# Two column tiles of 64 in place of each whole matmul, in a retention and MLP kernel

## The chip, the cores and the metric

The kernel runs on one core of one Trainium2 chip. The metric is the device time of one execution in microseconds. Before the change the median is 307.2 us of three runs (306.94 to 307.8). The executions compared here are of the fast state (granted TensorE clock 1.00), but for e8, whose single run has no state. The experiments ran on three chips (e1 to e4, e5 to e8, e9 to e12), each with its own rounds of the kernel before beside them. A profile's span is about 1.8 us shorter than the time of the same execution.

## The reference

```python
def _attn_ref(q, k, v):                     # 8 batches, 8 heads, 576 positions, 64 per head
    scores = 1/np.sqrt(64) * np.matmul(q, k.transpose(0, 1, 3, 2))
    gamma = 1.0 - 2.0 ** (-5.0 - np.arange(H))
    Dmat = np.where(rel >= 0, gamma[:, None, None] ** rel, 0.0)     # rel = i - j
    return np.matmul(scores * Dmat, v)

def _moe_ref(x, w_in, w_out):               # 4608 tokens, 512 -> 2048 -> 512
    h = x @ w_in
    return (h * (1 / (1 + np.exp(-1.702 * h)))) @ w_out
```

The output of the first, as 4608 rows of 512, is the input of the second. Inputs and output are float32; the kernel's matmuls are in bf16.

## The kernel before

TensorE does the matmuls and writes them to PSUM, a memory in banks; ScalarE and VectorE read the banks out, and the program lets a new group into a bank only after that. Each matmul has a weight load of its own. The rows are cut into 36 units of 128, and four units make a chunk of 512 columns for the MLP. For each unit TensorE does four things besides the MLP: `inter` (the running state times q), `scores` (k times q inside the unit), `values` (masked scores times v) and `state` (k times v, for later units). The MLP of a chunk has an *up* phase of 16 groups of four matmuls, each group followed by a gelu on ScalarE, and a *down* phase of 16 steps of four matmuls. The attention of later units is placed inside the MLP phases of earlier chunks.

```python
def state_mm(u, bank, first):
    # [cut]
    for hp in range(HP):                                  # HP = 4 pairs of heads
        op("pe", lambda e, hp=hp: e.matmul(
            kb[:, hp, :], kq[sl][:, 0, P * hp : P * hp + P],
            vp[u % NVP][:, 2 * hp : 2 * hp + 2, :],
            start=(first and hp == 0), stop=True, skip_group_check=True),
           reads=[f"kq{sl}_0", f"vp{u % NVP}"], writes=[bank])

def scores(u, sb0=None):                                  # contraction over 64 rows: row tiles
    # [cut]
            e.matmul(by_pair(bank)[:, hp, :], qt[64 * hh : 64 * hh + 64, hp, :],
                     qt[64 * hh : 64 * hh + 64, HP + hp, :], skip_group_check=True)

def values(u, first=False):                               # 64 outputs each: column tiles
    # [cut]
            e.matmul(ob[64 * hh : 64 * hh + 64, hp, :], vp[u % NVP][:, 2 * hp + hh, :],
                     pm[u % 4][hh][:, hp, :], ...)

def up(c, f):
    bank = f"H{count['up'] % 2}"                          # two PSUM banks in turn
    count["up"] += 1
    hb = banks[bank].ap()
    for a in range(HP):
        op("pe", lambda e, a=a: e.matmul(
            hb, w_in_sb[:, a, P * f : P * f + P], xT[c % 3][:, a, :],
            start=(a == 0), stop=(a == HP - 1)), ...)
    op("act", lambda e: e.activation(gT[c % 2][:, f, :], hb, AF.Gelu_apprx_sigmoid), ...)

def block(m):                                             # two units inside an MLP phase
    inter(a); inter(b)
    scores(a + 2); scores(b + 2)
    scores_out(a + 2, 0)
    values(a); values(b)
    # [cut: copies out of PSUM, later loads]
```

A matmul instruction addresses the whole 128x128 array, or a part of it: 64 rows and 128 columns (scores, two row tiles), or 128 rows and 64 columns (values, two column tiles). These are three tiling modes.

## Time and profile before

| | before |
|---|---|
| time, median | 307.2 us |
| span of the profiled execution | 305.3 us |
| TensorE busy (PE) | 299.5 us, 98% |
| ScalarE busy (ACT) | 121.3 us, 40% |
| TensorE waits for others, in all | 3.2 us, the last of them near 17 us |
| changes of tiling mode (counted in the trace) | 72 |

These lines are from the page of the kernel before: the line of busy times (us, share of the span, instructions), the chain that ended last by engine, and groups of instructions (line, engine, operation, tiles, shapes, count; then busy us, mean ns of one; then the idle time before them and its releaser). PEld is the weight loads.

```profile
PE 299.5 (98%) x2152; PEld 149.7 (49%) x2152; DVE 131.7 (43%) x277; ACT 121.3 (40%) x214; POOL 113.0 (37%) x139
...
PE 94%; POOL 3%; DMA 2%; issue 0%; ACT 0%; DVE 0%; POOLq 0%
...
L455 PE MATMUL psH<-xT,w_in_sb 128*128 128x512 bf16 x512 | 115.5, 379 | 0.0
L486 PE MATMUL psH<-w_out_sb,gT 128*128 128x512 bf16 x512 | 115.3, 379 | 0.0
L460 ACT ACTIVATE gT<-psH 128x512 bf16<-128x512 f32 x128 | 76.4, 597 | 49.3 <-PE psH L455 49.3
...
L455 PEld LDWEIGHTS psH<-xT,w_in_sb 128*128 128x128 bf16 x512 | 42.4, 97 | 62.6 <-ACT gT L460 22.8
```

A matmul of 379 ns counts as busy from its first read to its modelled end, so neighbours overlap and 98% says little. What counts is the distance between starts. Read from the single instructions of the trace, that distance inside one mode is 216 ns at N=512, 109 at 256, 56 at 128 and 29 at 64. At a change of mode it is about 95 ns more. The next lines are from the chain of waits in order of time (start us, length us, what), one usual block with the MLP round it: inter (L396), scores (L415), values (L434), MLP (L455).

```profile
161.72 0.45 PE psO L396 x8
162.17 0.55 PE psS L415 x16
162.72 0.57 PE psO L434 x16
163.29 1.83 PE psH L455 x8
165.12 4.32 PE psH L486 x20
```

Eight inter matmuls take 0.45 us, which is 56 ns each. Sixteen scores take 0.55 and sixteen values 0.57 us, of which eight pairs of 56 ns explain 0.45: the rest is the change into that mode. The first eight MLP matmuls take 1.83 us where 8 x 216 ns is 1.73: a third change.

Two of the waits of TensorE in this kernel, both in the head (who waited for whom, us in total, times, longest):

```profile
PE psS L415 <- ACT qkT L331: 0.7, 2, 0.3
...
PE psS L326 <- DMA kq<-in_k_dram: 0.3, 1, 0.3
```

And the weight loads of four groups of the last up phase (timeline, engine PEld: start us, length us, what, idle time before it and its releaser):

```profile
279.15 0.55 PEld L455 LDWEIGHTS psH<-xT,w_in_sb 128*128 128x128 bf16 x4 [0.32 <-ACT gT L460]
280.01 0.55 PEld L455 LDWEIGHTS psH<-xT,w_in_sb 128*128 128x128 bf16 x4 [0.32 <-ACT gT L460]
280.87 0.55 PEld L455 LDWEIGHTS psH<-xT,w_in_sb 128*128 128x128 bf16 x4 [0.32 <-ACT gT L460]
281.74 0.55 PEld L455 LDWEIGHTS psH<-xT,w_in_sb 128*128 128x128 bf16 x4 [0.32 <-ACT gT L460]
```

Each group of four begins with a load that waits for a gelu (L460), because the group's PSUM bank has to be read out first; the group period is 0.86 us, 4 x 216 ns.

### The profile page before, as it was taken

To read this page: it belongs to the slowest core of one execution; us is meant where nothing else is said; L and a number is where in the kernel's file an instruction comes from. 1 tells how busy PE (TensorE), PEld (TensorE's weight loads), DVE (VectorE), ACT (ScalarE), POOL (GpSimd) and SP (SyncE) were. 2 spreads that over 40 slices of the span, in tenths; PEclk is the share of its full clock that TensorE was granted. 3 is DMA by queue.
4 is the path that set the end of the run, shared out by engine and by line. 5 is a ranking of instruction groups with operands and counts; after the bars stand their busy time and mean duration, and the time that the engine had idled before them with its cause. 6 is when DMAs were issued, how large, how long until landed. Compare 5 with 4: busy or idle time off the path is not lost.

```text
span 305.3 us, 5121 instructions
## 1 busy us (share of the span) xinstructions
PE 299.5 (98%) x2152; PEld 149.7 (49%) x2152; DVE 131.7 (43%) x277; ACT 121.3 (40%) x214; POOL 113.0 (37%) x139
## 2 busy tenths in 40 slices
PE   8799999999999999999999999999999999999996
PEld 3444688445544444354445444545444544453344
DVE  5781860418453554245454544425452635210000
ACT  8566346211146213631363136412651165116611
POOL 9799920735336454260428015601562000000000
DMA  9999999999999999992699879985989510010022
GB/s 143 191 207 192 187 206 137 135 168 243 166 188 171 123 193 207 151 137 75 162 147 137 107 140 147 157 111 104 175 147 96 121 50 2 34 71 34 0 55 85
DMA packets 118119, 40.45 MB, mean 132 GB/s; under 512 B 107024, under 2 KB 111376, under 8 KB 118096
## 3 DMA queue, kind: packets, MB, share of 16 engines
q0 software_dynamic: 80016, 22.55, 68.5%
q1 hardware_dynamic: 38080, 17.57, 24.8%
q8 instruction: 17, 0.28, 0.4%
q14 instruction: 6, 0.05, 0.1%
HBM read 36.70 MB, written 9.44 MB: 151 GB/s over the span
## 4 chain that ended last, share of the span: by engine, by line
PE 94%; POOL 3%; DMA 2%; issue 0%; ACT 0%; DVE 0%; POOLq 0%
PE psH L486 37%; PE psH L455 36%; PE psH L472 5%; PE psO L434 3%; PE psS L415 3%; PE psS L348 2%; DMA vn<-in_v_dram 2%; PE psS L486 2%; POOL kq L203 2%; PE psO L396 2%; PE psO L486 1%; PE psS L312 1%; PE psS L512 1%; PE psO L512 1%; POOL vp L303 0%
## 5 line engine op out<-in xcount | busy, mean ns | idle before, releaser
L455 PE MATMUL psH<-xT,w_in_sb 128*128 128x512 bf16 x512 | 115.5, 379 | 0.0
L486 PE MATMUL psH<-w_out_sb,gT 128*128 128x512 bf16 x512 | 115.3, 379 | 0.0
L460 ACT ACTIVATE gT<-psH 128x512 bf16<-128x512 f32 x128 | 76.4, 597 | 49.3 <-PE psH L455 49.3
L217 POOL DMA_DIRECT2D vn<-in_v_dram x39 | 33.5, 870 | 115.2 <-DMA qkT<-kq 115.2
L486 PEld LDWEIGHTS psH<-w_out_sb,gT 128*128 128x128 bf16 x512 | 48.3, 98 | 56.4 <-ACT gT L460 1.9
L455 PEld LDWEIGHTS psH<-xT,w_in_sb 128*128 128x128 bf16 x512 | 42.4, 97 | 62.6 <-ACT gT L460 22.8
L494 ACT ACTIVATE osb<-psH 128x512 f32<-128x512 f32 x32 | 19.1, 597 | 106.7 <-PE psH L486 106.7
L424 DVE TENSOR_TENSOR pm<-psS,mask 128x512 bf16<-128x512 f32 x64 | 41.3, 684 | 44.9 <-PE psS L415 44.9
L203 POOL DMA_DIRECT2D kq<-in_q_dram x39 | 34.7, 899 | 0.0
L203 POOL DMA_DIRECT2D kq<-in_k_dram x39 | 34.5, 893 | 0.0
L444 DVE TENSOR_TENSOR xT<-psO,gq 128x512 bf16<-128x512 f32 x36 | 23.5, 684 | 12.2 <-PE psO L434 11.4
L378 DVE TENSOR_TENSOR kvf<-psS,kvf 64x256 f32<-64x256 f32 x24 | 10.1, 422 | 25.5 <-PE psS L348 25.3
L303 DVE TENSOR_TENSOR vp<-vn,vfac 128x512 bf16<-128x512 f32 x29 | 18.8, 688 | 0.2
L472 PE MATMUL psH<-xT,w_in_sb 128*128 128x256 bf16 x128 | 14.5, 273 | 0.0
L376 DVE COPY kvf<-psS 64x256 f32<-64x256 f32 x12 | 5.1, 422 | 20.0 <-PE psS L348 19.9
L477 ACT ACTIVATE gT<-psH 128x512 bf16<-128x512 f32 x16 | 9.6, 597 | 8.6 <-PE psH L472 8.6
L472 PEld LDWEIGHTS psH<-xT,w_in_sb 128*128 128x128 bf16 x128 | 11.8, 98 | 2.2 <-issue 0.2
L415 PE MATMUL psS<-qkT 64*128 64x128 bf16 x288 | 12.1, 218 | 0.7 <-ACT qkT L331 0.7
L434 PE MATMUL psO<-pm,vp 128*64 128x128 bf16 x288 | 12.2, 223 | 0.5 <-DVE vp L303 0.5
L518 DVE COPY osb<-psS 128x256 f32<-128x256 f32 x1 | 0.4, 425 | 28.4 <-PE psS L512 28.4
L348 PE MATMUL psS<-vp,kq 128*128 128x128 bf16 x128 | 12.4, 219 | 0.3 <-POOL vp L303 0.3
L348 PEld LDWEIGHTS psS<-vp,kq 128*128 128x128 bf16 x128 | 9.3, 98 | 6.9 <-ACT kv L361 0.7
(62 smaller groups left out, 147.5 us busy)
## 6 DMA issues: line engine op xcount, KB each, us to landing
vn<-in_v_dram POOLq DMA_DIRECT2D x31, 256.0 KB, 5.2
out_dram<-osb SPq DMA_DIRECT2D x31, 256.0 KB, 2.3
kq<-in_k_dram POOLq DMA_DIRECT2D x31, 128.0 KB, 5.7
kq<-in_q_dram POOLq DMA_DIRECT2D x31, 128.0 KB, 5.5
w_in_sb<-in_moe_w_in_dram POOLq DMA_DIRECT2D x4, 512.0 KB, 9.5
w_out_sb<-in_moe_w_out_dram POOLq DMA_DIRECT2D x4, 512.0 KB, 14.8
out_dram<-osb SPq DMA_DIRECT2D x10, 128.0 KB, 2.3
vn<-in_v_dram POOLq DMA_DIRECT2D x8, 128.0 KB, 4.0
```

What stands on the lines that cost most here:

```text
L203: e.dma_start(kq[sl][p0 : p0 + n, i, :].rearrange("p (h d) -> p h d", d=DH), src[b, :, s0 : s0 + n, :].rearrange("h p d -> p h d"),)
L217: e.dma_start(vn[sl][p0 : p0 + n, :, :], v[b, :, s0 : s0 + n, :].rearrange("h p d -> p h d"),)
L348: op("pe", lambda e, hp=hp: e.matmul(kb[:, hp, :], kq[sl][:, 0, P * hp : P * hp + P], vp[u % NVP][:, 2 * hp : 2 * hp + 2, :], start=(first ...
L415: op("pe", lambda e, hp=hp, hh=hh, bank=bank: e.matmul(by_pair(bank)[:, hp, :], qt[64 * hh : 64 * hh + 64, hp, :], qt[64 * hh : 64 * hh + ...
L424: op("dve", lambda e: e.tensor_tensor(pm[u % 4][hh].ap(), by_pair(bank), m[:, None, :].to_broadcast([P, HP, P]), ALU.mult), reads=[bank, " ...
L434: op("pe", lambda e, hp=hp, hh=hh: e.matmul(ob[64 * hh : 64 * hh + 64, hp, :], vp[u % NVP][:, 2 * hp + hh, :], pm[u % 4][hh][:, hp, :], st ...
L444: op("dve", lambda e: e.tensor_tensor(xT[ch % 3][:, :, 128 * j : 128 * j + 128], by_pair(bank), gq[:, ty, :, :], ALU.mult), reads=[bank] + ...
L455: op("pe", lambda e, a=a: e.matmul(hb, w_in_sb[:, a, P * f : P * f + P], xT[c % 3][:, a, :], start=(a == 0), stop=(a == HP - 1)), reads=[f ...
L460: op("act", lambda e: e.activation(gT[c % 2][:, f, :], hb, AF.Gelu_apprx_sigmoid), reads=[bank], writes=[f"gT{c % 2}_{f}"])
L472: op("pe", lambda e, a=a, f=f, j=j: e.matmul(hb[:, j, :], w_in_sb[:, a, P * f : P * f + P], xT[c % 3][:, a, n], start=(a == 0), stop=(a == ...
L486: op("pe", lambda e, f=f: e.matmul(y, gT[c % 2][:, f, P * r : P * r + P], w_out_sb[:, f, :], start=(f == 0), stop=(f == NF - 1)), reads=[f ...
L494: op("act", lambda e: e.activation(osb[o].ap(), y, AF.Copy), reads=[bank], writes=[f"osb{o}"])
```

## The change

The intent: let every matmul but the scores use the mode in which values stands anyway, 128 rows by 64 columns. Then the mode changes only on the way into scores and out of them. A whole matmul becomes two, one for each half of the output rows, which run side by side.

```diff
+        HALVES = (slice(0, 64), slice(64, 128))
+
+        def mm(y, lhs, rhs, reads, bank, start, stop=True, **kw):
+            for r in HALVES:
+                op("pe", lambda e, r=r: e.matmul(
+                    y[r], lhs[:, r], rhs, start=start, stop=stop, skip_group_check=True, **kw),
+                   reads=reads, writes=[bank])
@@ state_mm
             for hp in range(HP):
-                op("pe", lambda e, hp=hp: e.matmul(
-                    kb[:, hp, :], kq[sl][:, 0, P * hp : P * hp + P],
-                    vp[u % NVP][:, 2 * hp : 2 * hp + 2, :],
-                    start=(first and hp == 0), stop=True, skip_group_check=True),
-                   reads=[f"kq{sl}_0", f"vp{u % NVP}"], writes=[bank])
+                mm(kb[:, hp, :], kq[sl][:, 0, P * hp : P * hp + P],
+                   vp[u % NVP][:, 2 * hp : 2 * hp + 2, :],
+                   [f"kq{sl}_0", f"vp{u % NVP}"], bank, first and hp == 0)
@@ up
             for a in range(HP):
-                op("pe", lambda e, a=a: e.matmul(
-                    hb, w_in_sb[:, a, P * f : P * f + P], xT[c % 3][:, a, :],
-                    start=(a == 0), stop=(a == HP - 1)),
-                   reads=[f"win{f // 4}"] + [f"xT{c % 3}_{j}" for j in range(4)],
-                   writes=[bank])
+                mm(hb, w_in_sb[:, a, P * f : P * f + P], xT[c % 3][:, a, :],
+                   [f"win{f // 4}"] + [f"xT{c % 3}_{j}" for j in range(4)],
+                   bank, a == 0, a == HP - 1)
```

(The transposes, inter, the half-width up, the down matmuls and the warm-up are rewritten in the same way.)

More of the change, by code (lines that the diff above doesn't have):

```diff
@@ L311, in transpose_pe @@
             for j in range(2 * HP):
-                op("pe", lambda e, j=j: e.matmul(
-                    t[:, j, :], kq[sl][:, j // HP, P * (j % HP) : P * (j % HP) + P], ident.ap(),
-                    is_transpose=True), reads=[f"kq{sl}_{j // HP}", "ident"], writes=[bank])
+                mm(t[:, j, :], kq[sl][:, j // HP, P * (j % HP) : P * (j % HP) + P], ident.ap(),
+                   [f"kq{sl}_{j // HP}", "ident"], bank, True, is_transpose=True)
             if eng == "act":
@@ L325, in transpose_half @@
             for j in range(HP):
-                op("pe", lambda e, j=j: e.matmul(
-                    t[:, j, :], kq[sl][:, i, P * j : P * j + P], ident.ap(),
-                    is_transpose=True), reads=[f"kq{sl}_{i}", "ident"], writes=[bank])
+                mm(t[:, j, :], kq[sl][:, i, P * j : P * j + P], ident.ap(),
+                   [f"kq{sl}_{i}", "ident"], bank, True, is_transpose=True)
             dst = qkT[u % NQT][:, HP * i : HP * i + HP, :]
@@ L394, in inter @@
             for hp in range(HP):
-                if kind < 2:
-                    op("pe", lambda e, hp=hp: e.matmul(
-                        ob[:, hp, :], kv[kind][c - 1][:, hp, :], qt[:, HP + hp, :],
-                        start=(first and hp == 0), stop=True, skip_group_check=True),
-                       reads=[f"kv{kind}_{c - 1}_0", f"kv{kind}_{c - 1}_1", f"qkT{u % NQT}q"],
-                       writes=[bank])
-                else:
-                    for b in range(2):
-                        op("pe", lambda e, hp=hp, b=b: e.matmul(
-                            ob[:, hp, 64 * b : 64 * b + 64], kv[b][3][:, hp, :],
-                            qt[:, HP + hp, 64 * b : 64 * b + 64],
-                            start=(first and hp == 0 and b == 0), stop=True, skip_group_check=True),
-                           reads=[f"kv{b}_3_0", f"kv{b}_3_1", f"qkT{u % NQT}q"], writes=[bank])
+                for b in (kind,) if kind < 2 else (0, 1):
+                    n = slice(0, P) if kind < 2 else HALVES[b]
+                    x = c - 1 if kind < 2 else 3
+                    mm(ob[:, hp, n], kv[b][x][:, hp, :], qt[:, HP + hp, n],
+                       [f"kv{b}_{x}_0", f"kv{b}_{x}_1", f"qkT{u % NQT}q"], bank,
+                       first and hp == 0 and n.start == 0)
         def scores(u, sb0=None):
@@ L454, in up @@
             for a in range(HP):
-                op("pe", lambda e, a=a: e.matmul(
-                    hb, w_in_sb[:, a, P * f : P * f + P], xT[c % 3][:, a, :],
-                    start=(a == 0), stop=(a == HP - 1)),
-                   reads=[f"win{f // 4}"] + [f"xT{c % 3}_{j}" for j in range(4)],
-                   writes=[bank])
+                mm(hb, w_in_sb[:, a, P * f : P * f + P], xT[c % 3][:, a, :],
+                   [f"win{f // 4}"] + [f"xT{c % 3}_{j}" for j in range(4)],
+                   bank, a == 0, a == HP - 1)
             op("act", lambda e: e.activation(gT[c % 2][:, f, :], hb, AF.Gelu_apprx_sigmoid),
@@ L471, in up_half @@
                 for a in range(HP):
-                    op("pe", lambda e, a=a, f=f, j=j: e.matmul(
-                        hb[:, j, :], w_in_sb[:, a, P * f : P * f + P], xT[c % 3][:, a, n],
-                        start=(a == 0), stop=(a == HP - 1)),
-                       reads=[f"win{f // 4}"] + [f"xT{c % 3}_{2 * half + j}" for j in range(2)],
-                       writes=[bank])
+                    mm(hb[:, j, :], w_in_sb[:, a, P * f : P * f + P], xT[c % 3][:, a, n],
+                       [f"win{f // 4}"] + [f"xT{c % 3}_{2 * half + j}" for j in range(2)],
+                       bank, a == 0, a == HP - 1)
             op("act", lambda e: e.activation(
@@ L485, in down @@
             for f in range(4 * s, 4 * s + 4):
-                op("pe", lambda e, f=f: e.matmul(
-                    y, gT[c % 2][:, f, P * r : P * r + P], w_out_sb[:, f, :],
-                    start=(f == 0), stop=(f == NF - 1)),
-                   reads=[f"gT{c % 2}_{f}", f"wout{f // 4}"], writes=[bank])
+                mm(y, gT[c % 2][:, f, P * r : P * r + P], w_out_sb[:, f, :],
+                   [f"gT{c % 2}_{f}", f"wout{f // 4}"], bank, f == 0, f == NF - 1)
             if s < 3:
@@ L511, in down_last @@
                 for f in range(NF):
-                    op("pe", lambda e, f=f, y=y, c0=c0, c1=c1: e.matmul(
-                        y, gT[c % 2][:, f, P * r : P * r + P], w_out_sb[:, f, c0:c1],
-                        start=(f == 0), stop=(f == NF - 1)),
-                       reads=[f"gT{c % 2}_{f}", f"wout{f // 4}"], writes=[bank])
+                    mm(y, gT[c % 2][:, f, P * r : P * r + P], w_out_sb[:, f, c0:c1],
+                       [f"gT{c % 2}_{f}", f"wout{f // 4}"], bank, f == 0, f == NF - 1)
                 o = osb[r][:, c0:c1]
@@ L527, in warm @@
             for _ in range(n):
-                op("pe", lambda e: e.matmul(
-                    banks["H1"].ap(), zero[:, 0:P], zero.ap(), start=True, stop=True),
-                   reads=["zero"], writes=["H1"])
+                mm(banks["H1"].ap(), zero[:, 0:P], zero.ap(), ["zero"], "H1", True)
         def head_in(u, eng, bank="S2"):
```

## The prediction

> **What bounds the kernel now.** TensorE. The page's busy line gives PE 299.5 of 305.3 us (98%); the chain of waits is 94% PE; the view of waits shows PE waiting for others 3.2 us in all, none of it after 18 us. The granted clock is 1.00. So the time is the sum of PE's start-to-start intervals, read from the trace's single instructions. Inside one tiling mode they are 216 ns for a 128x512 matmul, 109 for N=256, 56 for N=128, 29 for N=64: nothing is left between matmuls except where the mode changes.
>
> **Mode changes.** The trace has 72 changes between 128x128, 64x128 (scores) and 128x64 (values). At each the first start comes about 95 ns later than the interval of that size (152 ns instead of 56 from the last values matmul to the first MLP matmul), and the next start another 10 to 20 ns late. This agrees with the Trainium skill, "TensorEngine Tiling (Array Packing)", Key Properties: a change of mode drains TensorE.
>
> **What the change removes.** Afterwards only the 22 groups of scores stand in another mode: 44 changes stay, 28 go. Four of the 28 lie before 16 us, where PE waits for a DMA anyway; 24 lie on the chain: 24 x (96 + about 10) ns = 2.5 us. The usual block (inter, scores, values, MLP) loses one change of three.
>
> **What it adds.** Matmuls go from 2152 to about 3,730, with as many weight loads. Column tiles do run side by side: the values pairs start 3 ns apart and follow each other every 56 ns, as whole matmuls with N=128 do. So I expect 216 ns per pair at N=512, 109 at 256, 56 at 128: no loss. The same page says that column tiling switches Fast Weight Load off; the trace shows 64-column loads of 110 ns against 98 ns for 128-column ones, hidden at N=128. The 32 matmuls with N=64 (29 ns) may not hide theirs: at worst 56 ns per pair, +0.9 us; I take +0.4. The other engines' work does not change.
>
> The unproved part is the supply of instructions. A period of 15.7 us needs about 384 PE instructions, 25 per us (18.5 inside the MLP), twice as many as before. The trace of before shows 320 in 12.7 us at the head; with a queue of 64 filled beforehand (the Trainium skill, "TensorE: Matmul & The Clock Gate", opening table) that proves at least 20 per us, an estimate. Capped near that, the kernel would be tens of us slower; I give this, or a loss between concurrent 512-column streams, one chance in eight.
>
> **Predicted:** 307.2 - 2.5 + 0.4 = 305.1 us, range 303.8 to 308.0. Faster by over 2%: 0.02; within 2%: 0.85; slower: 0.13.
>
> **What the profile would show.** Right: MLP matmuls as 128x64 pairs, starts 3 ns apart and 216 ns per pair; the first MLP start after values 56 ns after the last values pair, not 152; 44 mode changes of about 95 ns; a block (inter to first MLP matmul) of about 1.56 us instead of 1.66; weight-load busy time up; ACT and DVE busy times unchanged.
>
> **What would make it wrong.** Pairs over 216 ns at N=512 (weight loads no longer hidden, or two streams sharing a read path); gaps with no semaphore behind them (instruction supply); N=64 or transposed pairs well over 56 ns; a lower granted clock[...].

## The result, and the profile after

| | before | after |
|---|---|---|
| time, median (range) | 307.4 us (306.94 to 307.8, 4 runs) | 306.92 us (306.4 to 307.21, 4 runs) |
| ratio, 95% interval | | 0.9983 (0.9961 to 1.0005) |
| span of the profiled execution | 305.3 us | 305.4 us |
| matmuls | 2152 | 3728 |
| changes of tiling mode | 72 | 44 |

A ratio is the mean time of one kernel's fast runs over that of the other's of the same rounds, so it is not quite the ratio of the medians. About 0.5 us was gained; 2.1 us had been forecast. From the page after, the busy times and the chain:

```profile
PE 297.3 (97%) x3728; PEld 167.7 (55%) x3728; DVE 131.7 (43%) x277; ACT 121.4 (40%) x214; POOL 113.3 (37%) x139
...
PE 72%; DMA 15%; POOL 12%; issue 1%; DVE 0%; SPq 0%; POOLq 0%
...
```

From the groups by form of the kernel after (columns as above; line 313 is the helper, 456 the gelu):

```profile
L313 PE MATMUL psH<-xT,w_in_sb 128*64 128x512 bf16 x1024 | 116.4, 381 | 0.1
L313 PE MATMUL psH<-w_out_sb,gT 128*64 128x512 bf16 x1024 | 115.5, 379 | 0.0
L456 ACT ACTIVATE gT<-psH 128x512 bf16<-128x512 f32 x128 | 76.5, 597 | 49.6 <-PE psH L313 49.6
L313 PEld LDWEIGHTS psH<-xT,w_in_sb 128*64 128x64 bf16 x1280 | 63.1, 109 | 57.0 <-ACT gT L456 21.6 <-ACT osb L486 2.2 <-DVE xT L442 0.6
```

The down matmuls (`w_out_sb`) keep their mean of 379 ns, the up matmuls (`w_in_sb`) have 381: the first hint. The chain by engine looks quite different (72% PE, where it was 94%). That is no statement about shares of cost: one wait for a DMA at 84 us makes the walk back through the chain leave TensorE there and follow the loads before it. The usual block, from the chain of waits:

```profile
162.22 0.45 PE psO L313 x16
162.67 0.55 PE psS L413 x16
163.22 0.57 PE psO L432 x16
163.79 6.06 PE psH L313 x56
```

The 28 pairs of the MLP after values now take 6.06 us, where 28 x 216 ns is 6.05; before it was 1.83 + 4.32 = 6.15 us. The change of mode between values and MLP is gone, as forecast. In single instructions, the first MLP start comes 56 ns after the start of the last values pair (155 before; the prediction's 152 was counted from the pair's second matmul), and the block from its first inter to the first MLP matmul takes 1.568 us (1.663 before).

The waits of TensorE for loads of q and k after:

```profile
PE psS L313 <- DMA kq<-in_k_dram: 1.2, 2, 0.8
...
PE psS L413 <- DMA qkT<-kq: 0.6, 1, 0.6
...
PE psS L313 <- DMA kq<-in_q_dram: 0.2, 1, 0.2
```

The largest sum misleads: the two waits for k (1.2 us, where 0.3 was) stand at 7.8 and 13.0 us, and at 17 us this execution is only 0.06 us behind that of before. The two that cost time are new: 0.16 us of idle time for q of unit 4 at 28.2 us (the start there is 0.33 us late) and 0.57 us for the transposed q and k of unit 13 at 84.0 us (0.74 us late). And the weight loads of the last up phase:

```profile
279.12 0.57 PEld L313 LDWEIGHTS psH<-xT,w_in_sb 128*64 128x64 bf16 x8 [0.31 <-ACT gT L456]
279.99 0.57 PEld L313 LDWEIGHTS psH<-xT,w_in_sb 128*64 128x64 bf16 x8 [0.29 <-ACT gT L456]
280.87 0.57 PEld L313 LDWEIGHTS psH<-xT,w_in_sb 128*64 128x64 bf16 x8 [0.31 <-ACT gT L456]
281.73 0.57 PEld L313 LDWEIGHTS psH<-xT,w_in_sb 128*64 128x64 bf16 x8 [0.29 <-ACT gT L456]
```

The group starts are now 0.87, 0.88 and 0.86 us apart, and the idle time before them alternates between 0.31 and 0.29 us. The single instructions of the trace (times in us) show what happens at such a load:

```
                          weight load that     its matmul   the next     distance
                          waited for ScalarE   starts       matmul
before, a group           87.665               87.680       87.897       217 ns
after, a group            87.359, 87.362       87.365       87.600       235 ns
after, the next group     88.222, 88.225       88.248       88.464       216 ns
```

Of the 431 up intervals at N=512 after 54 us, 39 are more than 10 ns too long after the change, and none before.

**Where the time went, by anchors.** ScalarE executes the same 212 activations in the same order in both kernels. Comparing their starts gives the lag of one kernel against the other at any place. The table adds the later experiments; each row is one profile against the first profile of before.

| profile | to 87.0 us | 87.0 to 275.0 us | 275.0 us to the last | sum |
|---|---|---|---|---|
| after | +0.56 | -0.62 | +0.16 | +0.09 |
| after, second profile (e1) | +0.39 | -0.62 | +0.16 | -0.08 |
| after, more banks (e2) | +0.56 | -1.23 | +0.02 | -0.65 |
| before, more banks (e3) | +0.42 | 0.00 | 0.00 | +0.42 |
| after, loads reordered (e4) | +0.02 | -0.62 | +0.15 | -0.44 |
| after, whole head (e5) | 0.00 | -0.62 | +0.16 | -0.46 |
| before, warm-up cut (e6) | +0.40 | 0.00 | 0.00 | +0.40 |
| whole head and more banks (e7) | -0.16 | -1.23 | +0.02 | -1.37 |
| after, last up whole (e8) | +0.54 | -0.62 | +0.23 | +0.15 |
| e7 with inter whole (e10) | +0.07 | +0.12 | +0.02 | +0.21 |
| e7 with state whole (e11) | +1.08 | +3.53 | +0.02 | +4.63 |
| e7 with loads reordered (e12) | +0.11 | -1.23 | +0.02 | -1.10 |

From 87 us on the numbers repeat to 10 ns from profile to profile; up to there (the head) kernels with the very same TensorE instructions differ by 0.4 us. Those 0.4 us are there at 17 us already: from 17 to 87 us e3 and e6 repeat the kernel before to 0.03 us, and only the kernels with column tiles differ, by -0.41 (e7) to +0.50 us (after), e10 and e11 with their added changes left aside. The second table splits the time from 86 us to the end by the distances between starts, in us.

| profile | changes of mode | cost of them, with the start after | late MLP starts |
|---|---|---|---|
| before | 35 | 3.89 | 0.00 |
| after | 22 | 2.51 | 0.85 |
| e2 | 22 | 2.51 | 0.13 |
| e10 | 35 | 3.90 | 0.13 |
| e11 | 64 | 7.26 | 0.13 |

The late starts that stay in e2 are those of the first down matmuls, which wait for a gelu too. So after 86 us 13 changes of mode went and saved 3.89 - 2.51 = 1.38 us, 106 ns each, exactly the price in the prediction; and 0.85 us of it was lost again in the MLP.

### The profile page after: what moved, and what is told of

Same layout as the page of the kernel before. It is cut to its first block, busy times and chain, and to the rows that moved or that the text cites. A ratio compares the mean times of both kernels' runs of the same rounds, so it can differ in the third digit from the quotient of the medians.

```text
span 305.4 us, 8273 instructions
## 1 busy us (share of the span) xinstructions
PE 297.3 (97%) x3728; PEld 167.7 (55%) x3728; DVE 131.7 (43%) x277; ACT 121.4 (40%) x214; POOL 113.3 (37%) x139
## 4 chain that ended last, share of the span: by engine, by line
PE 72%; DMA 15%; POOL 12%; issue 1%; DVE 0%; SPq 0%; POOLq 0%
PE psH L313 60%; DMA kq<-in_q_dram 9%; POOL kq L203 6%; PE psS L313 4%; DMA qkT<-kq 3%; POOL vn L217 3%; PE psO L313 3%; PE psO L432 2%; DMA vn<-in_v_dram 2%; PE psS L413 2%; POOL vp L303 1%; POOL w_out_sb L232 1%; POOL w_in_sb L226 0%; POOL iota_c L238 0%; DVE osb L508 0%
## 5 line engine op out<-in xcount | busy, mean ns | idle before, releaser
L313 PE MATMUL psH<-xT,w_in_sb 128*64 128x512 bf16 (+1 forms) x1280 | 131.0, 359 | 0.1
L313 PE MATMUL psH<-w_out_sb,gT 128*64 128x512 bf16 x1024 | 115.5, 379 | 0.0
L313 PEld LDWEIGHTS psH<-xT,w_in_sb 128*64 128x64 bf16 x1280 | 63.1, 109 | 57.0 <-ACT gT L456 21.6
L313 PEld LDWEIGHTS psH<-w_out_sb,gT 128*64 128x64 bf16 x1024 | 56.1, 110 | 48.6 <-ACT gT L456 1.9
L313 PEld LDWEIGHTS psS<-vp,kq 128*64 128x64 bf16 x256 | 10.3, 110 | 5.9 <-ACT kv L366 0.7
L413 PE MATMUL psS<-qkT 64*128 64x128 bf16 x288 | 12.2, 218 | 1.4 <-ACT qkT L338 0.7
L313 PE MATMUL psS<-vp,kq 128*64 128x128 bf16 x256 | 12.6, 220 | 0.2 <-POOL vp L303 0.2
L389 DVE TENSOR_TENSOR kv<-psS,kvf 64x256 bf16<-64x256 f32 x12 | 5.1, 422 | 16.2 <-PE psS L313 16.1
L386 DVE CAST kv<-kvf 64x256 bf16<-64x256 f32 x36 | 11.4, 317 | 1.2
```

The source lines that it names most:

```text
L313: op("pe", lambda e, r=r: e.matmul(y[r], lhs[:, r], rhs, start=start, stop=stop, skip_group_check=True, **kw), reads=reads, writes=[bank])
L386: op("dve", lambda e, d=dst, s=acc: e.tensor_copy(d, s), reads=[kfk, f"kv{kind}_{c}"], writes=[kvk])
L413: op("pe", lambda e, hp=hp, hh=hh, bank=bank: e.matmul(by_pair(bank)[:, hp, :], qt[64 * hh : 64 * hh + 64, hp, :], qt[64 * hh : 64 * hh + ...
```

## The experiments

My theory after reading the traces had two parts. W: in the up phase a group's first weight load waits for a gelu, and a 64-column load must stand longer ahead of its matmul than a whole one, so that a wait which had just been hidden shows. H or D: the head, up to about 84 us, is set by loads and copies, so that what TensorE saves there turns into waiting. The rival S: twice as many instructions are not supplied fast enough, or the two streams of a pair disturb each other.

**e1, the changed kernel again.** No edit.

> The changed kernel, unaltered, for a second profile and a tighter ratio. Three accounts of the 2 us that the prediction missed. (W) In the up phases a group's first weight load waits for the gelu of two groups earlier; a 64-column load needs about 25 ns before its matmul, a whole one about 13, and only about 15 ns of slack were there, so every second group of the seven later up phases loses 20 ns: I expect start intervals of about 235 ns again, some 30 to 55 of them, 0.6 to 1.1 us. (D) Loads from memory: the first profile had a 0.74 us wait for the transposed q and k of units 12 and 13 near 83 us and 0.33 us near 28 us. If this is the change's own doing, both waits stand here again at like size; if it is run-to-run scatter of the DMA, they move by several tenths. (S, rival) shortage of instructions: gaps at random places in the MLP and not only behind the wait for the gelu. Ratio to before 0.997 to 1.000.

Measured: 307.01 us (306.85 to 307.48), ratio 0.9987 (0.9974 to 1.0000). The same number of late up intervals, 39, 0.74 us in sum. All other intervals of one mode from 86 us on, about 1,180 of them, add up to 0.07 us more than at the lengths that they have in before: no random gaps, so S is out as far as supply is concerned. The waits for loads moved: 0.91 us near 28 us, and none near 83 us. So W repeats exactly, and the load waits are scatter in place and size.

**e2, more PSUM banks for the later up phases.**

```diff
+        UPB = ["H0", "S0", "S2", "S3"] + ["H0", "H1", "S2", "S3"] * 2 + ["H0", "H1", "H0", "H1"]
             bank = f"H{count['up'] % 2}"
+            if c >= 2:
+                bank = UPB[f]
```

> The changed kernel with the later up phases spread over more PSUM banks (H0, H1 and the score banks free at that time), so that no group's first weight load waits for a gelu. W expects all up intervals at 216 ns (none of 230 to 240), and 0.6 to 1.1 us less than the changed kernel. S or a conflict between the two streams expects the 235 ns intervals to stay and no gain.

Measured: 306.40 us (306.06 to 307.27), ratio 0.9971 (0.9959 to 0.9984), against 0.9987 for e1 on the same chip. One late up interval is left of 39. In the trace the time from 87 us on falls by 0.74 us against e1, within what W expected; in the medians it is 0.6. The weight loads of this kernel in the same stretch (timeline, PEld) and its chain in the last up phase, with the eight pairs before it:

```profile
279.13 1.62 PEld L313 LDWEIGHTS psS<-xT,w_in_sb 128*64 128x64 bf16 x16
280.86 1.62 PEld L313 LDWEIGHTS psH<-xT,w_in_sb 128*64 128x64 bf16 x16
```

```profile
272.61 2.59 PE psH L313 x24
275.20 2.59 PE psS L313 x24
277.79 1.73 PE psH L313 x16
279.51 1.73 PE psS L313 x16
281.24 1.73 PE psH L313 x16
282.97 1.73 PE psS L313 x16
284.69 3.48 PE psH L313 x32
```

The same 72 pairs in the chain of before and of after:

```profile
273.17 1.83 PE psH L486 x8
275.01 13.81 PE psH L455 x64
```

```profile
273.21 15.70 PE psH L313 x144
```

The seven lines of e2 add to 15.58 us, the theoretical 72 x 216 ns being 15.55. Before needs 1.83 + 13.81 = 15.64 (with its change of mode after values), after 15.70. That is the whole case in three sums: the change of mode was removed and more than its price was lost again; with free banks the loads no longer wait (no idle time is shown, and 16 of them run on as one row) and the gain stays. A conflict between the two streams of a pair would not have gone away with the bank.

**e3, the same banks in the kernel before.** The edit is that of e2, applied to the kernel before.

> The kernel before with the same extra banks. Its up phases already run at 216 ns throughout, so W expects no change: within 0.1 us (0.03 per cent) of before, apart from scatter. If it gains as much as the changed kernel does, the lost time is not due to column tiles.

Measured: 307.49 us (307.06 to 307.61), ratio 0.9997 (0.9985 to 1.0009); 0.00 us in the trace from 87 us to the end. The waiting load costs nothing with whole tiles, so the loss belongs to the column tiles.

**e4, the loads of q and k of units 12 and 13 ahead of those of v.**

```diff
-            (0, 5): [lambda: ready_t(5), lambda: fetch((10, 11, 12, 13), (12, 13), 10)],
+            (0, 5): [lambda: ready_t(5), lambda: fetch((10, 11), (12, 13), 10),
+                     lambda: fetch((12, 13), (), 10)],
```

> The changed kernel with the loads of q and k for units 12 and 13 issued ahead of those of v for the same units (two v loads, about 1.8 us of issue, moved behind them). D expects the transposes of units 12 and 13 one to two us earlier and the wait near 83 us gone: up to 0.7 us less than the changed kernel in runs that had the wait. If the wait is scatter that is mostly absent, the gain is below 0.2 us.

Measured: 307.29 us, but from 306.62 to 308.31; ratio 0.9996 (0.9981 to 1.0011). The transposes of unit 13 were issued at 77.4 us, against 80.9 and 79.7 in the two profiles of the changed kernel, and the wait near 83 us is absent. The times do not show a gain, and their scatter is larger than in any other run. Inconclusive in time. The wait itself looks like this in the timeline of before and then of after (two groups of eight scores, L415 and L413):

```profile
82.55 0.61 PE L396 MATMUL psO<-qkT,kv 128*128 128x128 bf16 x8
83.10 0.62 PE L415 MATMUL psS<-qkT 64*128 64x128 bf16 x16
83.65 0.64 PE L434 MATMUL psO<-pm,vp 128*64 128x128 bf16 x16
```

```profile
83.01 0.40 PE L413 MATMUL psS<-qkT 64*128 64x128 bf16 x8
83.98 0.40 PE L413 MATMUL psS<-qkT 64*128 64x128 bf16 x8 [0.57 <-DMA qkT<-kq]
84.30 0.47 PE L432 MATMUL psO<-pm,vp 128*64 128x128 bf16 x10
```

In before the scores of both units run on as sixteen; in after the second unit's start 0.97 us after the first's, 0.57 of it charged to the DMA transpose. Of eleven profiles with the old order of loads (the slow one left out), three showed such a wait (after, e2, e8) and eight did not, five of which have column tiles there (e1, e5, e7, e10, e11).

**e5, whole matmuls in the head.** The helper takes a flag, which falls after the eighth group of the first up phase, near 26 us.

```diff
+        whole = [True]
-            for r in HALVES:
+            for r in ((slice(0, P),) if whole[0] else HALVES):
         play(16, lambda f: up(0, f), {
+            7: [lambda: whole.__setitem__(0, False)],
```

> The changed kernel with whole 128x128 matmuls until about 26 us (through the eighth group of the first up phase), column tiles from there on. Head theory (H): before about 28 us the time is set by loads and copies, so the changes of mode removed there save nothing; and twice the instructions bring one more 16 KB fetch of instructions, at 22.4 us instead of 33.6, in the middle of the loads of unit 4, whose last piece then lands 0.4 to 0.7 us late. H expects fetches near 17 and 28 to 34 us, no wait for the load of unit 4 near 28 us (0.33 and 0.91 us in the two profiles of the changed kernel), and 0.2 to 0.8 us less than the changed kernel. The rival, that the landing scatters whatever the kernel, expects no gain.

Measured: 306.84 us (306.64 to 307.17), ratio 0.9983 (0.9971 to 0.9996): not to be told from the changed kernel (0.9983 and 0.9987). The fetches of instructions moved to 17.2 and 33.4 us, as expected. But the last piece of unit 4's load still landed at 28.39 us, 0.9 us behind the piece before it. So the fetch at 22 us is not what makes that piece late: this part of H falls. And 0.6 us went to a wait for a weight matrix near 19 us instead. That the head gains nothing from the tiles is supported; that it loses by them is not.

**e6, more instructions in the head of the kernel before.**

```diff
             for _ in range(n):
-                op("pe", lambda e: e.matmul(
-                    banks["H1"].ap(), zero[:, 0:P], zero.ap(), start=True, stop=True),
+                cuts = (0, 96, 192, 288, 384, 512) if n in (10, 3) else (0, 128, 256, 384, 512)
+                for c0, c1 in zip(cuts, cuts[1:]):
+                    op("pe", lambda e, c0=c0, c1=c1: e.matmul(
+                        banks["H1"][:, c0:c1], zero[:, 0:P], zero[:, c0:c1], ...
```

> The kernel before, its warm-up matmuls cut into four or five pieces of the same total width: same TensorE time, 170 more instructions at the head, so that a fetch of instructions falls near 22 to 23 us, as in the changed kernel. If such a fetch delays the load of unit 4, its last piece lands 0.3 to 0.9 us after TensorE asks for it near 28 us, and the kernel is up to 0.6 us slower than before. If the landing only scatters, no wait (it was absent in both profiles of kernels with whole matmuls) and no loss beyond 0.1 us.

Measured: 307.68 us (307.46 to 308.52), ratio 1.0016 (1.0003 to 1.0028). A fetch stood at 22.0 us, and the load of unit 4 landed at 28.02 us, 0.18 us before TensorE asked: no wait. The 0.4 us of this profile were lost before 17 us, as in e3, where nothing was added to the head. With e5 this ends the idea of the fetch. Over the ten profiles up to e8, with before and after, the last piece of that load landed between 27.70 and 28.78 us, with and without a fetch near 22 us, and TensorE asks, or without the wait would have asked, near 27.8 to 28.4 us. Here is the place in before and in after (timeline; L312 and L313 are the transposes of unit 4):

```profile
27.65 0.61 PE L312 MATMUL psS<-ident,kq 128*128 128x128 bf16 x8
```

```profile
27.69 0.39 PE L313 MATMUL psS<-ident,kq 128*64 128x128 bf16 x8
28.24 0.41 PE L313 MATMUL psS<-ident,kq 128*64 128x128 bf16 x8 [0.16 <-DMA kq<-in_q_dram]
28.49 0.60 PE L313 MATMUL psH<-xT,w_in_sb 128*64 128x512 bf16 x4
```

In before the eight transposes run on; in after the second four, which need q, start 0.55 us after the first four.

**e7, both mends.** The edits of e2 and e5 together.

> Both mends at once: whole matmuls until 26 us and the later up phases on more banks. If the two losses add, 1.0 us (extra banks) less than e5 is too much: I expect 0.6 us below e5, and 305.4 to 306.2 us in all, against 307.4 before.

Measured: 305.83 us (305.64 to 305.94), ratio 0.9950 (0.9937 to 0.9964). This is 1.0 us below e5 in the medians, more than the 0.6 expected. The trace from 87 us on has 0.75 us of it; the rest is the head, 0.16 us lower than in e5. It beats both kernels, by 1.6 and by about 1.1 us.

**e8, whole matmuls in the last up phase alone.** The flag of e5, set only for the last up phase; two banks, as in the change.

> The changed kernel with whole matmuls in the last up phase alone (two PSUM banks as before), column tiles elsewhere. If the 20 ns come from the longer start of a 64-column weight load behind the wait for the gelu, all 16 groups of that phase run at 216 ns, against eight intervals of 230 to 235 and several of 219 in the changed kernel, and two changes of mode of about 100 ns each come in at its ends: 46 changes of mode. If the wait itself were at fault, the 235 ns stay.

Measured: 307.24 us in one run, of unknown state, so only its profile counts. All recorded starts of that phase are 215 to 217 ns apart (two matmuls have no record), where the changed kernel has eight of 232 to 235 ns and five of 217 to 220; 46 changes of mode. The phase and its two ends cost 0.23 us, against 0.16 in the change and 0.02 in e2. So the wait for the gelu alone does no harm; it is the wait together with the 64-column load.

**e9, e7 again, as a base.** No edit.

> The kernel of e7 once more, as the base of this call: 305.5 to 306.0 us, 53 changes of mode.

Measured: 305.80 us median; the four fast runs lie between 305.27 and 305.89, ratio 0.9945 (0.9931 to 0.9958). The fifth, profiled, was the slow one.

**e10, inter whole again.**

```diff
+        def mm(y, lhs, rhs, reads, bank, start, stop=True, one=False, **kw):
-            for r in ((slice(0, P),) if whole[0] else HALVES):
+            for r in ((slice(0, P),) if whole[0] or one else HALVES):
@@ inter
-                       first and hp == 0 and n.start == 0)
+                       first and hp == 0 and n.start == 0, one=True)
```

> The kernel of e7 with the inter matmuls whole again: about 21 changes of mode more (one at each of 14 blocks, two at the last and at three units of the head). If a change costs about 105 ns on the chain, as single instructions show, 1.8 to 2.3 us more than e9_again. If the drains are partly hidden, or the records exaggerate them, under 1 us.

Measured: 307.62 us (307.29 to 307.92), ratio 1.0013 (0.9999 to 1.0026). There are 74 changes of mode, 21 more than in e7. The mean of its runs is 2.0 us above that of e9's fast runs, or 96 ns a change. In the trace, 13 changes more from 87 us on cost 1.35 us, 104 ns each.

**e11, state whole again.** The same flag in `state_mm` alone.

> The kernel of e7 with the state matmuls whole again: 50 to 56 changes of mode more, two round nearly each of 28 states, within stretches where TensorE waits for nothing. At 105 ns each 5 to 6 us more than e9_again, about 311 us, slower than the kernel before. Together with e10 this is a dose: time against the number of changes.

Measured: 311.76 us (311.73 to 312.01, 4 runs), ratio 1.0147 (1.0133 to 1.0161), with 106 changes. The mean is 6.2 us above e9's fast runs for 53 more, 117 ns each; in the trace from 87 us on it is 4.76 us for 42, 113 ns each. The time rises with the count of changes, and at the price read from the single instructions, wherever TensorE waits for nothing else.

**e12, e7 with the loads of e4.** Both edits stand above.

> The kernel of e7 with q and k of units 12 and 13 loaded ahead of v. The wait near 83 us stood in three of the six profiles of the changed kernel and its variants with the old order (0.74, 0.29, 0.43 us) and not in e5 or e7. If it is scatter at an edge, the earlier load removes it in the runs that have it: 0 to 0.3 us less than e9_again in the median.

Measured: 305.88 us (305.73 to 306.22), ratio 0.9956 (0.9943 to 0.9968), against 305.80 for e9. No gain; the wait near 83 us is absent, but it was absent in e7 too, and this profile waits for another load of q instead, 0.64 us at 35.3 us. The earlier load is not worth keeping on this evidence.

## Why the prediction was right or wrong

- **Bound by TensorE's starts: right from 86 us on, wrong before.** It rested on a view of waits that shows only 3.2 us. But a wait that is zero says nothing of the slack behind it: in the profile of before, the load of unit 4 landed at 27.705 us, for a weight load at 27.817.
- **Column tiles run side by side at no cost: right.** Nearly all pairs start 1 to 5 ns apart (sixteen with N=256, near 47 us, about 30), and they follow each other every 216, 109 and 56 ns at N=512, 256 and 128.
- **28 changes go, 44 stay; 96 + 10 ns each: right.** 44 were counted, and the 13 removed after 86 us saved 106 ns each. The Trainium skill's "TensorEngine Tiling (Array Packing)", Key Properties (a change of mode drains TensorE), agrees with this and with e10 and e11.
- **"24 lie on the chain": this step failed.** 13 did. The other 11 lie between 16 and 86 us. They did save their price of starts there, 1.15 to 1.18 us, but TensorE then reached other work before it was ready, and waits took the time back. Counted by single starts in the five profiles with tiles from the beginning (after, e1, e2, e4, e8): about 0.4 us came back each time in longer waits for copies near 17.5, 19 and 37 us (0.5 in e4), about 0.2 us in late starts behind loads that had waited, and 0.26 to 1.07 us in waits for loads of q and k, at other places from profile to profile (0.33 us near 28 and 0.74 near 84 us in after, 0.91 us near 28 in e1). The lag gained from 17 to 87 us is -0.12 to +0.50 us in these five, against 0.00 to 0.03 with whole matmuls (e3, e6); with the head whole up to 26 us (e5, e7, e12) it is -0.41 to +0.21. No dependable gain came out of the head.
- **"The same page says that column tiling switches Fast Weight Load off ... hidden at N=128": right at N=128, and the step that it stood for, no loss in the MLP, failed.** Where a load waits for a gelu it is not hidden. From 86 us on, 71 such loads of the up phases began 15 to 16 ns ahead of their matmul in before, and the next start lost 1 ns at most. In after 39 began 6 to 10 ns ahead and lost 15 to 20 ns; 32 began 22 to 27 ns ahead and lost 4 ns at most. After a change of mode, where a load starts 1 to 5 ns ahead of its matmul, the loss is 10 ns for whole and 24 ns for 64-column loads. So a whole load wants about 15 ns and a 64-column load about 25 ns, an estimate from these sums of lead and loss. In before the loop of two banks, 597 ns of gelu and the signals round it left 15 ns. Every second group now loses about 20 ns; the loss of one leaves slack for the next. That term was missing from the sum: 0.85 us from 86 us on.
- **+0.4 us for the 32 matmuls with N=64: too much.** Their pairs follow each other every 31 ns, the whole ones every 29. From 86 us on that is 0.05 us.
- **Supply of instructions: no shortage.** In one stretch of the changed kernel 420 TensorE instructions start within 9.3 us; less the queue of 64 from the Trainium skill's page "TensorE: Matmul & The Clock Gate" (opening table) this proves at least 38 per us, an estimate; 25 were needed.
- **The clock** stayed at 1.00.

The sum, corrected: -1.38 us (changes of mode after 86 us) + 0.85 (late MLP starts) + 0.07 (the other intervals, 0.05 of it the pairs with N=64) + about 0 (the head, scatter of 0.4 us) = -0.46 us. The table of anchors has -0.62 + 0.16 = -0.46, and the ratios 0.9983 and 0.9987 of 307.4 us stand for -0.5 and -0.4 us.

Open: why the last piece of a load comes up to 0.9 us after the others in some executions. The fetch of instructions does not explain it. Whether the tiles make the head slightly worse (e7 against e2: 0.7 us in the head, 0.4 of it after 17 us, in one profile each) was not separated from this scatter. What in a 64-column load, or in loading two of them, takes the 10 ns more is not shown either.

## What to carry to other kernels

Before you split matmuls to save changes of tiling mode, list the weight loads that wait for a semaphore, and measure how many nanoseconds they start ahead of their matmul: here a column-tiled load needed about 10 ns more, and a loop that was just hidden showed it in every second turn, until it got more PSUM banks. Price a removed stall only where TensorE has no other wait close behind; an idle time of zero in a profile does not tell how near the next load was. Where the two conditions hold, a change had a steady price in this kernel: 96 to 117 ns each, added or removed.

## What the Trainium skill lacked or had wrong

- "TensorEngine Tiling (Array Packing)", Key Properties, says that a change of mode drains TensorE and gives no price. Here the first start is about 95 ns late and the next 10 to 24 ns; 96 to 117 ns per change in the dose of e10 and e11.
- The same page, Restrictions, says that column tiling disables Fast Weight Load, and not when that costs. Here it costs nothing at N=128 to 512 while loads run ahead, 2 ns a pair at N=64 (31 ns, where a whole matmul has 29), and about 10 ns of lead where a load waits; together with two PSUM banks in turn that became 20 ns in every second group.
- "TensorE: Matmul & The Clock Gate", LDWEIGHTS, gives a load P / 1.2 ns for P columns, so 53 ns for 64 and 107 for 128. As a rate this does not hold here: with N=64 two 64-column loads go by every 31 ns in after, and one whole load every 29 ns in before. The recorded durations are 110 and 98 ns.
- The same page, Back-to-back issue gap, gives a sustained 131 ns per matmul at N=512 and 81 at N=128, weight loads included. Here it is 216 and 56 ns, with a weight load for each: the values that this section gives for an isolated matmul.
- The same page, Part 3, says that a weight load overlaps matmuls in flight only in other row groups (Part 2, and another passage of Part 3, allow a background buffer as well). Here loads start 1 to 2 ns after a matmul over the same 128 rows has started, in both kernels.
